# A fused attention and feed-forward kernel: attention-times-value matmuls of four head groups in one run, with attention weights reloaded per chunk

## The chip, the cores and the metric

The kernel runs on one core of a Trainium2 chip. The metric is the device time of one execution in microseconds (us); a figure for a kernel is the median of several executions. TensorE has two kinds of records in the traces, matmuls (PE) and weight loads (PEld).

## The reference

```python
# x [1, 2048, 576]; wqkv [576, 1728]; wo [576, 576]; w_gate, w_up [576, 4608]; w_down [4608, 576]; all bf16
xn = layernorm(x)
# A: 32 heads of 18, each query sees itself and the 255 keys before it
q, k, v = split(xn @ wqkv)
p = softmax(where(mask, q @ k.T * 18**-0.5, -1e9))
s = (p @ v) @ wo
# B: gated feed-forward
g = silu((sigmoid(xn @ w_gate) * (xn @ w_up)) @ w_down)
return x + s * g
```

## The kernel before

A host-side scheduler builds a list of operations per engine, simulates it with estimated durations and emits it unrolled: every matmul is an instruction of its own, there is no loop on the chip. The sequence of 2048 rows is cut into four chunks of 512. Attention (scores, exp, mask, then the product of probabilities and values, "PV") is fitted between the feed-forward matmuls, which are most of the work. Nearly all matmuls come in pairs that run at once, one on each row half of the array (in the trace of the kernel before, the two start 3 ns apart in the median, and at 512 columns the next pair starts 0.216 us later):

```python
def pair(eng, outs, lhs, rhs, start, stop, swap=0):            # L118
    for i in range(2):
        t = i ^ swap
        res = eng.matmul(outs[i], lhs(ROWS[t], i), rhs(ROWS[t], i), start=start, stop=stop, tile_position=(64 * t, 0))
```

Heads come in eight groups of four. A PV run takes two groups and one PSUM unit. Its matmuls use smaller tiles, 64 rows by 32 columns, eight at once (in the run at 163.89 us the eight of the first step start within 23 ns, and the next step 142 ns after the first's start):

```python
def build_pv(self, c, pr):                                     # L779, cut
    hp = self.pool_s.hold()                                    # one PSUM unit
    def f_pv(eng):
        outs = self.halves(hp, NT)
        for n, ks in enumerate(kss):                           # 12 key sub-blocks, 8 in chunk 0
            q0, q1 = span[ks]                                  # 1 to 5 query sub-blocks of 64
            cols = slice(q0 * SW, q1 * SW)
            for g, (hg, where, _) in enumerate(pend):          # 2 head groups
                for t in range(2):
                    for i in range(2):
                        res = eng.matmul(outs[i][p0:p0 + VH, cols], self.v_aug[ROWS[i], o:o + VH],
                                         self.expr[ROWS[i], se, t, cols], start=n == 0, stop=n == len(kss) - 1,
                                         tile_position=(64 * i, p0), skip_group_check=True)
    # ... then per half: transpose from PSUM, reciprocal, product, transpose back, DMA to oT
```

So a run is 12 x 8 = 96 matmuls in chunks 1 to 3 and 64 in chunk 0, with nothing else between them. There are 16 runs. The attention weights are loaded once and stay.

The softmax here doesn't subtract the row's maximum and nothing guards it: scores larger than these inputs give would overflow.

## Time and profile before

| | before |
|---|---|
| time, median (lowest to highest) | 559.01 us (558.83 to 559.52), 3 runs |
| span of the profiled run, granted clock | 557.7 us, 1.00 |
| PE busy | 552.4 us |
| next busiest engine (DVE) | 333.6 us |

The prediction below shows the lines that carry the reading of this profile. Two more views matter later. The first is the chain of work that ended last, in order of time (columns: start us, length us, engine, line, count). L801 is PV and L122 is `pair`.

```profile
163.96 1.27 PE ps L801 x89
165.23 22.82 PE ps L122 x246
188.05 1.27 PE ps L801 x87
```

A run passes through the chain in one piece, and the next feed-forward pair follows at once. The second view is the page's list of DMA queues (columns: packets, MB, share of 16 engines):

```profile
q1 hardware_dynamic: 105960, 60.68, 39.7%
q0 software_dynamic: 7424, 5.92, 4.0%
q8 instruction: 66, 1.08, 0.8%
```

Queue q8 is of the kind "instruction": 66 packets of 1.08 MB / 66 = 16.4 KB each.

### The profile page before, as it was taken

How to read it: one execution, taken by the hardware profiler on the slowest of the kernel's cores; microseconds unless marked ns; L12 is line 12 of the kernel's file. 1: busy time of each engine (PE TensorE's matmuls, PEld its weight loads, DVE VectorE, ACT ScalarE, POOL GpSimd, SP SyncE). 2: the span in 40 equal slices, each digit the busy share in tenths (PEclk: the TensorE clock that was granted, in tenths of full speed). 3: DMA queues.
4: the chain of work that ended last, by engine and by line, in shares of the span. 5: the costliest groups of instructions: out<-in, count | busy, mean ns of one | idle time of the engine just before them, and what ended most of it. 6: DMA issues, size and time to landing. Idle time of an engine off the chain costs nothing.

```text
span 557.7 us, 19262 instructions
## 1 busy us (share of the span) xinstructions
PE 552.4 (99%) x8342; PEld 339.1 (61%) x8342; DVE 333.6 (60%) x797; ACT 274.3 (49%) x383; POOL 210.3 (38%) x360
## 2 busy tenths in 40 slices
PE   8999999999999999999999999999999999999997
PEld 7454444677755545457886555645588754444787
DVE  5477788787568667674558757357567623333133
ACT  4245654443656655645656464565756433223011
POOL 5564456566245454440667434034382200000000
PEclk9999999999999999999999999999999999999999
DMA  7988997831125535534121264234511035552010
GB/s 217 323 234 190 223 264 211 213 58 45 53 73 155 159 108 145 142 108 96 29 63 44 72 192 123 82 117 140 171 31 38 24 115 148 169 151 68 2 45 24
DMA packets 113468, 67.83 MB, mean 122 GB/s; under 512 B 18620, under 2 KB 111516, under 8 KB 113384
## 3 DMA queue, kind: packets, MB, share of 16 engines
q1 hardware_dynamic: 105960, 60.68, 39.7%
q0 software_dynamic: 7424, 5.92, 4.0%
q8 instruction: 66, 1.08, 0.8%
q14 instruction: 18, 0.15, 0.1%
HBM read 55.15 MB, written 2.36 MB: 103 GB/s over the span
## 4 chain that ended last, share of the span: by engine, by line
PE 98%; DVE 1%; DMA 0%; issue 0%; DVEq 0%
PE ps L122 95%; PE ps L801 3%; DMA x<-in_A_x_dram 0%; DVE small L525 0%; DVE small L527 0%; DVE xnr L541 0%; PE ps L599 0%; DVE s_attn L1062 0%; DVE thf L1067 0%; DVE xnr L545 0%; DVE small L529 0%; DVE small L531 0%; DVE xf L1072 0%; DVEq L1227 0%
## 5 line engine op out<-in xcount | busy, mean ns | idle before, releaser
L122 PE MATMUL ps<-xnT,wgs 64*128 64x512 bf16 (+1 forms) x2400 | 282.6, 368 | 0.2
L751 ACT ACTIVATE expr<-ps 128x1024 bf16<-128x1024 f32 (+4 forms) x160 | 154.9, 969 | 77.8 <-PE ps L122 77.2
L122 PEld LDWEIGHTS ps<-xnT,wgs 64*128 64x128 bf16 x2400 | 113.9, 94 | 115.0 <-DVE hT L949 1.6
L122 PE MATMUL ps<-wd_sb,hT 64*128 64x288 bf16 (+2 forms) x2448 | 156.7, 276 | 0.0
L949 DVE SCALAR_TENSOR_TENSOR hT<-tring,ps 128x512 bf16<-128x512 bf16 x144 | 98.3, 683 | 94.7 <-ACT tring L946 93.6
L946 ACT ACTIVATE tring<-ps 128x512 bf16<-128x512 f32 x144 | 86.1, 598 | 129.6 <-PE ps L122 127.5
L122 PEld LDWEIGHTS ps<-wd_sb,hT 64*128 64x128 bf16 x2448 | 112.5, 94 | 28.5
L279 POOL DMA_DIRECT2D qk<-qd x160 | 82.2, 521 | 119.9 <-PE ps L122 109.6
L764 DVE TENSOR_TENSOR expr<-expr,mask 128x128 bf16<-128x128 bf16 (+2 forms) x240 | 63.6, 299 | 62.3 <-ACT expr L751 61.7
L715 POOL TENSOR_SCALAR kx<-kprev,small 128x256 bf16<-128x256 bf16 x64 | 61.3, 967 | 28.2 <-PE ps L122 27.4
L122 PE MATMUL ps<-qk,kx 64*128 64x320 bf16 (+1 forms) x704 | 59.4, 254 | 0.0
L279 POOL DMA_DIRECT2D oT<-o2T x72 | 36.4, 513 | 58.7 <-DVE o2T L827 49.8
L122 PE MATMUL ps<-xnT,wgr 64*128 64x512 bf16 (+1 forms) x300 | 56.0, 367 | 0.0
L122 PEld LDWEIGHTS ps<-qk,kx 64*128 64x128 bf16 x704 | 31.2, 94 | 21.5 <-ACT expr L751 0.6
L122 PE MATMUL ps<-xnT,wqk 64*128 64x512 bf16 x256 | 32.6, 376 | 0.0
L1052 ACT ACTIVATE thf<-ps 128x576 bf16<-128x576 f32 (+3 forms) x22 | 11.4, 519 | 39.7 <-PE ps L122 39.4
L819 DVE STREAM_TRANSPOSE ot<-ps 128x512 f32<-128x512 f32 x32 | 22.4, 700 | 11.6 <-PE ps L801 11.5
L715 DVE TENSOR_SCALAR kx<-qk,small 128x512 bf16<-128x512 bf16 x64 | 22.4, 378 | 4.7 <-PE ps L122 4.1
L122 PEld LDWEIGHTS ps<-xnT,wgr 64*128 64x128 bf16 x300 | 14.9, 94 | 16.5
L827 DVE STREAM_TRANSPOSE o2T<-o 128x512 bf16<-128x512 bf16 x32 | 22.7, 711 | 1.0
L637 DVE CAST qd<-ps 128x1024 bf16<-128x1024 f32 (+1 forms) x20 | 22.1, 1111 | 1.5 <-PE ps L122 1.5
L697 ACT ACTIVATE v_aug<-ps 64x288 bf16<-64x288 f32 x32 | 13.1, 409 | 17.3 <-PE ps L122 16.8
(71 smaller groups left out, 300.9 us busy)
## 6 DMA issues: line engine op xcount, KB each, us to landing
wgs<-in_B_w_gate_dram SPq DMA_DIRECT2D x72, 256.0 KB, 3.3
wgs<-in_B_w_up_dram SPq DMA_DIRECT2D x72, 256.0 KB, 3.9
wd_sb<-in_B_w_down_dram SPq DMA_DIRECT2D x9, 576.0 KB, 6.3
qk<-qd POOLq DMA_DIRECT2D x100, 36.0 KB, 2.6
wgr<-in_B_w_gate_dram SPq DMA_DIRECT2D x36, 64.0 KB, 2.3
wgr<-in_B_w_up_dram SPq DMA_DIRECT2D x36, 64.0 KB, 2.7
xf<-in_A_x_dram SPq DMA_DIRECT2D x16, 144.0 KB, 2.6
out_dram<-xf SPq DMA_DIRECT2D x15, 144.0 KB, 1.8
```

The costliest lines, as they stand in the source:

```text
L122: res = eng.matmul(outs[i], lhs(ROWS[t], i), rhs(ROWS[t], i), start=start, stop=stop, tile_position=(64 * t, 0))
L279: o = self.op(eng, DMA_ISSUE_NS[eng], lambda e: e.dma_start(dst, src), name, deps, prio, nbytes=nbytes)
L637: return eng.tensor_copy(dst, self.both(h, n))
L697: return eng.activation(dst, src, ACTF.Copy)
L715: return e.tensor_scalar(self.kx[:, sx, pos:pos + n_ // SW, t, :], src.rearrange("p (s k) -> p s k", k=SW), self.half[:, t:t + 1], None, A ...
L751: return eng.activation(self.expr[:, se, :, lo * SW:NT], self.both(h, NT)[:, :, lo * SW:NT], ACTF.Exp, scale=SM_SCALE)
L764: return eng.tensor_tensor(e_, e_, m_, ALU.mult)
L801: res = eng.matmul(outs[i][p0:p0 + VH, cols], self.v_aug[ROWS[i], o:o + VH], self.expr[ROWS[i], se, t, cols], start=n == 0, stop=n == len( ...
L819: return e.transpose(self.ot1[:, p1, :], self.halves(hp, NT)[i])
L827: t2 = op("DVE", dve_ns(NT), lambda e, p2=p2, p3=p3: e.transpose(self.o2T[:, p3, :], self.o2[:, p2, :]), f"ot2:{c}:{pr}:{i}", deps=[on, d3 ...
L946: th = op("ACT", act_ns(NT), lambda e: e.activation(self.tring[:, st, :], bank(h, 0), ACTF.Tanh, scale=0.5), f"th:{c}:{ft}", deps=[pg, dt_ ...
L949: mu = op("DVE", dve_ns(NT), lambda e: e.scalar_tensor_tensor(self.hT[:, ft, :], self.tring[:, st, :], 1.0, bank(h, 1), ALU.add, ALU.mult) ...
```

## The change

The intent is to halve the number of PV runs, because TensorE loses about a quarter of a microsecond around each (0.214 us in chunk 0 and 0.265 us later, read from the trace of the kernel before). Four head groups need 20 exp buffers in place of 12. The room comes from keeping only small buffers for the attention weights, reloading them in each chunk, and normalizing in place. The spacing of the score visits was tuned anew.

```diff
-NEX = 12
+NEX = 20
+NWQ = 2
+PVG = 2
-NQD = 2
+NQD = 1
+EVAC = (1, 0)
-SPACE_NS = ((1500, 1500, 1400, ...
+SPACE_NS = ((2200, 1700, 1500, ...
 ... (cut: buffers)
-        self.wqk, _ = seq("wqk", [P, KB - 1, 2, D])
-        self.wv_sb, _ = seq("wv_sb", [P, KB - 1, D])
-        self.wo_sb, _ = seq("wo_sb", [P, KB - 1, D])
+        self.wqk, _ = seq("wqk", [P, NWQ, KB - 1, 2, P])
+        self.wvo, _ = seq("wvo", [P, KB - 1, D])
 ... (cut: the remainders of these buffers)
-        self.xr, _ = seq("xr", [P, NXR, D])
 ... (cut: loads of q/k per column group, of v and o per chunk, LN in place)
-        if hg % 2:
-            self.build_pv(c, hg // 2)
+        if hg % (2 * PVG) == 2 * PVG - 1:
+            self.build_pv(c, hg // 2 - PVG + 1)
 ...
-        hp = self.pool_s.hold()
+        hp = self.pool_s.hold(PVG)
+        hps = hp.split()
 ...
-            outs = self.halves(hp, NT)
-            for n, ks in enumerate(kss):
+            for u, n, ks in [(u, n, ks) for u in range(PVG) for n, ks in enumerate(kss)]:
+                outs = self.halves(hps[u], NT)
-                for g, (hg, where, _) in enumerate(pend):
+                for g, (hg, where, _) in enumerate(pend[2 * u:2 * u + 2]):
```

There are now eight PV runs of 192 matmuls (128 in chunk 0).

## The prediction

> **What bounds the kernel now.** I read the page first: the busy shares, then the chain that ended last.

> ```profile
> PE 552.4 (99%) x8342; PEld 339.1 (61%) x8342; DVE 333.6 (60%) x797; ACT 274.3 (49%) x383; POOL 210.3 (38%) x360
> ...
> PE 98%; DVE 1%; DMA 0%; issue 0%; DVEq 0%
> PE ps L122 95%; PE ps L801 3%; DMA x<-in_A_x_dram 0%; DVE small L525 0%; DVE small L527 0%; DVE xnr L541 0%; PE ps L599 0%; DVE s_attn L1062 0%; DVE thf L1067 0%; DVE xnr L545 0%; DVE small L529 0%; DVE small L531 0%; DVE xf L1072 0%; DVEq L1227 0%
> ```

> The chain is TensorE from 7.3 us to 554.6 us; the next engine is busy only 60%. But the matmuls' recorded times overlap (the groups give a 512-column matmul 376 ns, the sum of all would exceed the span), so "99%" does not say that the array streams all the time. I therefore looked at starts. This is the timeline of TensorE around one PV run of a later chunk (columns: start us, length us, engine, line, operation, count):

> ```profile
> 162.93 0.81 PE L122 MATMUL ps<-xnT,wgs 64*128 64x512 bf16 x6
> 163.58 0.38 PE L122 MATMUL ps<-xnT,wgr 64*128 64x512 bf16 x2
> 163.89 1.34 PE L801 MATMUL ps<-expr,v_aug 64*19 64x320 bf16 x96
> 165.16 0.34 PE L122 MATMUL ps<-qk,kx 64*128 64x64 bf16 x4
> ```

> and around one of the first chunk:

> ```profile
> 63.00 0.59 PE L122 MATMUL ps<-xnT,wgs 64*128 64x512 bf16 x4
> 63.44 0.38 PE L122 MATMUL ps<-xnT,wgr 64*128 64x512 bf16 x2
> 63.74 1.01 PE L801 MATMUL ps<-expr,v_aug 64*19 64x320 bf16 x64
> 64.69 0.31 PE L122 MATMUL ps<-qk,kx 64*128 64x320 bf16 x2
> ```

> What to see: from 162.93 to 163.58 there are three pairs (the two of a pair run at once), so a 512-column pair takes 0.216 us start to start, that is 512 columns at 0.417 ns and 2.5 ns more. Taking this price for every pair in the trace, I summed how much later each next matmul starts than it could. Outside the PV runs, after the first 10 us, only about 1 us is left over in the whole span (two gaps of 0.23 us at 22.8 and 45.3 us are the largest). The array is full; time can only come from work that is itself less, from gaps at the PV runs, or from the start.

> **The gaps at the PV runs.** In a later chunk the pair before the run ends its turn at 163.58 + 0.216 = 163.796; the score matmul after it starts at 165.16: 1.364 us. The run has 12 steps, each of 8 matmuls at once, with 64 x (1+2+3+4+5+5+5+5+4+3+2+1) = 2560 columns: 2560 x 0.417 + 12 x 2.5 ns = 1.10 us. So 0.265 us is overhead: 0.094 at the entry (163.89 - 163.796), the rest inside and at the exit (I read about 0.142 at the exit, 0.03 within). In chunk 0 there are 8 steps and 1920 columns, 0.82 us of stream, and 64.69 - 63.656 = 1.034 us of time: 0.214 of overhead, 0.093 and 0.116 of it at the ends. Sixteen runs lose 4 x 0.214 + 12 x 0.265 = 4.0 us.

> [...] PV uses 64 rows x 32 columns (outputs of 19 partitions at 0, 32, 64, 96), all else 64 x 128. [...] one such change in, one out, 0.21 to 0.24 us together, and no such gap between other matmuls. [...] in this trace no run is held up measurably (the waits list TensorE's weight loads of L801 at 3.3 us of "issue" in 10 cases, at most 0.4[...] and 1.5 us on the mask line L764). [...] By the allocations, the kernel before takes 212.7 KB, about 207.7 KiB[...]. [...] the records here show 34 ns mean for a 256 B packet, 29 for 512 B, 59 for 1152 B: small packets cost over twice as much per byte.

> **The change part by part.**
> PV in one run on two units: the same matmuls, 8 runs in place of 16. Each merge takes away one exit and one entry, 0.21 us in chunk 0 (2 merges) and 0.235 us later (6 merges): 0.42 + 1.41 = 1.83 us, all of it on the path, since TensorE is the path. The 0.03 us inside a run stays.
> Twenty exp buffers: 8 more of 2048 B, 16.4 KB. Freed: q/k, v and o weights 22.0 KB, the raw x tiles 2.3 KB, half of qd 2.0 KB; new: small q/k buffers 4.6 KB and one v/o buffer 5.2 KB. Net 16.6 KB. It just fits. But four head groups have 4 x 5 = 20 visits: there is no spare buffer now (12 against 10 before). Visit 21 waits for the PV run, PV for the last exp (1.02 us) and its mask (0.3 to 0.43), and for both score units; after it both units need two transposes of 0.70 us with a normalization between (2.15 us for one transpose, reciprocal, product, transpose back). So at each of the 8 merges scores stand still for an estimated 4 to 6 us. This is covered by feed-forward matmuls, provided there are any: after the last PV run at 440 us there are 114 us of pure L122, so the attention runs a whole chunk ahead, and slowing it by 8 x 5 us moves nothing at the end. The wider spacing sums likewise: 5 visits x (54.4 - 49.0) us = 27 us more attention, well under 114.
> Reloads: 2.6 MB once becomes four times, 8.0 MB more on 67.8; q/k columns now in 256 and 128 B rows. Per chunk some 5900 small packets x 34 ns and 1280 others x 54 ns are 270 us of engine time, 17 us of 16 engines; four chunks less the 9 us of before is an estimated 58 us, spread over 450 us. The share goes from about 45% to some 55%. Off the path where the transfer is asked for early.
> Issues on the SP queue: some 100 more at about 0.55 us, hidden. LN in place, one qd buffer, one v/o buffer: added ordering, no added engine work; five small DVE copies go. No TensorE work is added.
> Sum: 559.0 - 1.8, plus an allowance of 0.1 us in four or so places where a wait now shows, gives 557.3.

> **The rivals.**
> (1) New waits at the PV run eat the gain. Both score units, one of which also serves the feed-forward, are held together for the run (2.3 us) and for up to two normalizations. Then feed-forward has two units: each takes 1.94 us of matmuls (9 pairs), and its tanh (0.60) and product (0.69) plus a possible transpose ahead on DVE (0.72) take 2.3 us with the hops. That would stall TensorE up to 0.4 us a few times per merge, 3 to 6 us in all, and the time would be 558 to 562. Against it: before, scores and PV also occupied both units around a run and no stall shows.
> (2) Weights late in the first 100 us. The windows show the transfers there near their ceiling (columns: window, length, busy us and count of PE, PEld, DVE, ACT, POOL, clock, DMA share, GB/s):

> ```profile
> 20.00:40.00 20.00, 19.93 (x218) 10.28 (x216) 12.30 (x28) 6.73 (x14) 9.95 (x21) 1.00 1.00 275
> 40.00:60.00 20.00, 19.93 (x202) 9.38 (x200) 16.21 (x49) 10.95 (x17) 7.73 (x14) 1.00 0.77 176
> 60.00:80.00 20.00, 20.00 (x266) 9.98 (x262) 16.21 (x45) 11.64 (x18) 12.20 (x21) 1.00 1.03 256
> ```

> Chunk 0 now fetches q/k in short rows there, about 8 us more of DMA time over 90 us. For it: 1.00 of share. Against: the first 40 us ask for fewer bytes than before (two of five column groups in place of all), and the shares stay under what the queue carried at 323 GB/s in one slice. Worth +1 to +3 us if it comes.
> (3) The gain is larger than the drain, because wider spacing also removes the remaining small gaps. There is only about 1 us of them: 556 at best.

> **Range and chances.** Faster by over 2% would need 547.8, which nothing here can give with a full array; slower by over 2% would need 11 us of stalls, more than rivals 1 and 2 in their middle size. The range 555.8 to 559.6 takes in the full drain with some small gaps below, and rival 1 or 2 at a third of its size above.

> **What would show it.** Right: 8 groups of 192 (128 in chunk 0) matmuls of L801 in the chain, each about 2.45 us long (1.85 in chunk 0), TensorE otherwise without gaps, the mean spacing unchanged, attention ending later than 440 us, some 76 MB moved. Wrong: gaps of 0.1 us or more ahead of L801 or of feed-forward pairs just after it, waited for on DVE lines L764, L819 or L949, would be rival 1; gaps ended by weight transfers before 110 us would be rival 2. The prediction is also wrong if the change of tile between the two halves of a merged run drains too, for then no time is saved at all.

Where passages are cut, the cut is marked: they gave rules and a figure that no trace or run shows. 559.0 - 1.83 for the eight merges, plus 0.1 us for waits that show, gives 557.3 us; the 1.83 us are worked out from the measured 0.21 and 0.235 us per merge. That the buffers' room is used up, the reason given for freeing some, was not shown; the sum of 16.4 KB needed and 16.6 KB freed stands without it. "Drain", in the prediction and in the expectations, is the time lost where the tiles change, and the traces show that time alone.

## The result, and the profile after

| | before | after |
|---|---|---|
| time, median (lowest to highest), same chip | 559.08 us (558.83 to 559.52), 4 runs | 573.65 us (573.24 to 574.92), 4 runs |
| span of the profiled run, granted clock | 557.7 us, 1.00 | 572.0 us, 0.997 |

The ratio is 1.0264, with a 95% interval of 1.0246 to 1.0282: slower by 2.6%. The prediction of 557.3 us, with a range up to 559.6, was wrong.

First the page of the kernel after (busy times, DMA totals, the main queue and the chain by engine). L823 is PV and L129 is `pair`:

```profile
PE 554.1 (97%) x8342; PEld 348.8 (61%) x8342; DVE 331.2 (58%) x792; ACT 273.7 (48%) x383; POOL 209.0 (37%) x360
...
DMA packets 141341, 75.87 MB, mean 133 GB/s; under 512 B 43804, under 2 KB 139388, under 8 KB 141256
...
q1 hardware_dynamic: 133832, 68.71, 44.9%
...
PE 96%; issue 2%; DVE 1%; DMA 0%; DVEq 0%
```

The number of matmuls is the same, 8342, and PE is busy for nearly the same time. What is new is "issue", 2% of the chain: time in which TensorE waited for nothing that the profile shows. The chain in order of time shows where it lies (columns as before):

```profile
135.47 1.79 PE ps L823 x124
137.26 0.23 PE ps L129 x2
137.49 1.47 issue
138.96 63.82 PE ps L129 x740
202.78 1.72 PE ps L823 x118
204.50 2.01 issue
206.51 0.90 PE ps L823 x48
207.40 2.07 PE ps L129 x17
```

The run at 202.78 is broken in two by 2.01 us of nothing. The timeline of TensorE there (columns: start us, length us, engine, line, operation, count, idle time before) puts numbers on it:

```profile
202.39 0.38 PE L129 MATMUL ps<-xnT,wgr 64*128 64x512 bf16 x2
202.71 1.79 PE L823 MATMUL ps<-expr,v_aug 64*19 64x320 bf16 x137
206.51 0.90 PE L823 MATMUL ps<-expr,v_aug 64*19 64x256 bf16 x55 [2.01 <-issue]
207.33 1.04 PE L129 MATMUL ps<-xnT,wgs 64*128 64x512 bf16 x8
```

The 137th matmul starts at 204.23 (its neighbours overlap it, so the row's length is longer) and the 138th at 206.51. Nothing in the program separates these two; they are of one kind, in one run, and the program waits for all their data before the run, not inside it. The waits of TensorE (columns: engine and line, what was waited for, us in total, times, longest) sum up the whole span:

```profile
PE ps L823 <- issue: 10.0, 6, 2.8
PE ps L129 <- issue: 2.0, 2, 1.5
```

Six runs of eight stop inside, and one, the second of chunk 0, just behind its end (137.49). Only the first run has none. Taking the starts of matmuls (the method of the prediction), and a run's 0.205 us of overhead without a stop (measured in e2_align below), the seven stops cost 1.65, 2.23, 0.73, 2.50, 2.94, 1.32 and 1.65 us: **13.0 us**. (The expectations below count the idle time between records instead, 11.4 us.)

### A theory: the program does not arrive in time

What do seven places have in common, when none of them waits for data? I numbered TensorE's instructions in program order: one for every weight load, matmul and semaphore record. The kernel after has 16,941 of them, and q8 has 66 packets: 256.7 instructions to a packet. The other kernels agree: e2_align below has 18,033 instructions and 70 packets (257.6), e6_before_dense 19,721 and 77 (256.1). So I counted in blocks of 256.

In this numbering **all seven stops lie at place 192 or 193 of 256**. Since that one place holds for all, it is taken as the block's end; the first 64 instructions of the first block would then be ones without a record, which is an inference. From here on "crossing" is TensorE reaching such a place. These are the times of the stops in the kernel after, with the start of the q8 packet that comes between:

```
crossing   next crossing reached   q8 packet starts   TensorE goes on
 135.40          137.19                136.58              138.96
 202.85          204.23                204.03              206.51
 255.15          256.58                254.92              257.36
 313.62          315.02                314.95              317.36
 369.55          371.09                371.43              374.05
 436.02          437.39                436.46              438.79
 487.96          489.40                488.17              491.10
```

By the theory the density of the instructions decides. Each matmul is two instructions, its weight load and itself (8342 of each on the page). A feed-forward pair is four in 0.216 us, so 256 last 13.8 us. A PV run is 384 instructions in 2.40 us, so 256 last 1.6 us. Before, a run was 192 instructions: any 256 that held a whole run held at least 64 others too, 2.0 to 3.5 us of feed-forward (pairs of 288 or of 512 columns). Merging two runs made 384 in a row. By the theory a run that holds two crossings stops; the experiments test that.

### The rest of the difference

After the stop at 315 us the granted clock fell. This is the table of windows (columns: window, length, busy us and count of PE, PEld, DVE, ACT, POOL, clock, DMA share, GB/s):

```profile
315.00:317.30 2.30, 0.29 (x30) 0.10 (x10) 0.00 (x0) 0.00 (x0) 0.02 (x1) 1.00 0.38 108
317.36:318.30 0.94, 0.94 (x53) 0.84 (x52) 0.00 (x0) 0.00 (x0) 0.00 (x0) 0.79 0.00 0
318.37:321.60 3.23, 3.23 (x25) 1.12 (x18) 2.39 (x5) 0.60 (x1) 0.00 (x0) 0.54 0.02 5
321.60:325.00 3.40, 3.33 (x36) 1.47 (x34) 2.86 (x6) 1.22 (x2) 0.00 (x0) 1.00 0.06 16
```

In the third window seven feed-forward pairs took 0.40 to 0.43 us each in place of 0.216: 2.96 - 7 x 0.216 = 1.45 us. In each of the eleven traces all changes of the clock lie whole multiples of 3.413 us apart, and the half clock here lasts 3.413 us, from 317.91 to 321.32. Cut into windows on that grid, the traces have, inside their spans, six windows (in four traces) in which TensorE was idle for 1.92 to 2.51 us by its records, and each was followed by a window at half clock; no window with up to 1.89 us was. So in these traces it depends on where a stop falls. The one at 315 us lay in one window (2.07 us idle), the longer one at 371 us was cut by a window's end (1.24 and 1.52 us) and was followed by 1.00.

The sum, before to after: stops +13.03, half clock +1.45, the first 11 us +1.19 (of which 0.69 is a gap at instruction 449, again place 193 of 256; in the kernel before the first 11 us have 1.75 us of gaps, here 2.94), the runs' tile changes -1.86. That is 13.81 of the 572.04 - 557.68 = 14.36 us between the two profiles. The other 0.55 us are small waits.

### The profile page after: what moved, and what is told of

Same layout as the page of the kernel before. It is cut to its first block, busy times and chain, and to the rows that moved or that the text cites. A ratio compares the mean times of both kernels' runs of the same rounds, so it can differ in the third digit from the quotient of the medians.

```text
span 572.0 us, 19381 instructions
## 1 busy us (share of the span) xinstructions
PE 554.1 (97%) x8342; PEld 348.8 (61%) x8342; DVE 331.2 (58%) x792; ACT 273.7 (48%) x383; POOL 209.0 (37%) x360
## 2 busy tenths in 40 slices
DMA packets 141341, 75.87 MB, mean 133 GB/s; under 512 B 43804, under 2 KB 139388, under 8 KB 141256
## 3 DMA queue, kind: packets, MB, share of 16 engines
q1 hardware_dynamic: 133832, 68.71, 44.9%
## 4 chain that ended last, share of the span: by engine, by line
PE 96%; issue 2%; DVE 1%; DMA 0%; DVEq 0%
PE ps L129 92%; PE ps L823 3%; DMA x<-in_A_x_dram 0%; DVE small L523 0%; DVE small L525 0%; PE ps L595 0%; DVE xnr L539 0%; DVE s_attn L1086 0%; DVE thf L1091 0%; DVE xnr L543 0%; DVE small L527 0%; DVE small L529 0%; DVE xf L1096 0%; DVEq L1251 0%
## 5 line engine op out<-in xcount | busy, mean ns | idle before, releaser
L129 PE MATMUL ps<-xnT,wgs 64*128 64x512 bf16 (+1 forms) x2400 | 287.0, 369 | 0.8 <-issue 0.5
L129 PEld LDWEIGHTS ps<-xnT,wgs 64*128 64x128 bf16 x2400 | 117.7, 94 | 111.9 <-issue 3.9
L129 PE MATMUL ps<-wd_sb,hT 64*128 64x288 bf16 (+2 forms) x2448 | 155.1, 276 | 1.5 <-issue 1.5
L129 PEld LDWEIGHTS ps<-wd_sb,hT 64*128 64x128 bf16 x2448 | 114.4, 94 | 28.9 <-issue 1.7
L129 PE MATMUL ps<-qk,kx 64*128 64x320 bf16 (+1 forms) x704 | 59.9, 254 | 0.0
L129 PE MATMUL ps<-xnT,wgr 64*128 64x512 bf16 (+1 forms) x300 | 56.8, 369 | 0.0
L129 PEld LDWEIGHTS ps<-qk,kx 64*128 64x128 bf16 x704 | 33.2, 94 | 24.1 <-ACT expr L776 0.9
L129 PE MATMUL ps<-xnT,wqk 64*128 64x512 bf16 (+1 forms) x320 | 37.8, 355 | 0.1
L1076 ACT ACTIVATE thf<-ps 128x576 bf16<-128x576 f32 (+3 forms) x22 | 11.4, 520 | 50.0 <-PE ps L129 49.7
L823 PE MATMUL ps<-expr,v_aug 64*19 64x320 bf16 (+4 forms) x1408 | 19.9, 255 | 10.0 <-issue 10.0
L744 POOL COPY kprev<-qk 128x256 bf16<-128x256 bf16 x32 | 12.6, 401 | 38.2 <-DVE kx L740 36.9
L823 PEld LDWEIGHTS ps<-expr,v_aug 64*19 64x19 bf16 x1408 | 17.3, 87 | 14.1 <-issue 12.3
L129 PEld LDWEIGHTS ps<-xnT,wgr 64*128 64x128 bf16 x300 | 15.5, 94 | 16.1 <-issue 0.3
```

Source lines behind the costliest of these rows:

```text
L744: self.op_kp[hg] = op("POOL", 420, lambda e: e.tensor_copy(self.kprev[:, hg, :], self.qk[:, qs, 1, NT // 2:NT]), f"kp:{c}:{hg}", deps=[kxo ...
L1076: return e.activation(v2(t)[:, a:b, :], y2()[:, a:b, :], ACTF.Tanh, scale=0.25)
```

## The experiments

All results were correct. The runs e1 to e4 share a before of 558.87 us, e5 to e7 one of 558.89, e8 and e9 one of 558.95. To move crossings without moving data, an edit called padding below splits some feed-forward pairs into two halves over their columns, well ahead of a PV run. That adds four instructions per pair and hardly any array time, and shifts all that follows by four places:

```diff
+    if SPLIT[0] and not start:
+        SPLIT[0] -= 1
+        n = outs[0].shape[-1] // 2
+        for a in (0, n):
+            for i in range(2):
+                t = i ^ swap
+                res = eng.matmul(outs[i][:, a:a + n], lhs(ROWS[t], i), rhs(ROWS[t], i)[:, a:a + n],
+                                 start=False, stop=stop and a > 0, tile_position=(64 * t, 0))
+        return res
```

Places below are a run's first instruction, modulo 256, in the numbering of above (crossing at 192).

### e1_pvg1: the change without the merge

```diff
-PVG = 2
-EVAC = (1, 0)
+PVG = 1
+EVAC = (0,)
```

> The changed kernel with its PV runs cut back to two head groups on one PSUM unit; 20 exp buffers, reloads, in-place LN and new spacing stay. Theory F (TensorE's program arrives in blocks of 256 instructions, and a run of 384 instructions in 2.2 us uses a block up faster than the next one comes): the seven stops (11.4 us) and the eight slow pairs (1.7 us) go, eight drains (1.8 us) come back: 560 to 563 us, no idle time of over 0.4 us inside or just behind a PV run. Rival B (both PSUM units and all 20 exp buffers held by one run make waits): falls too, this run does not tell B from F. Rival D (the reloads and the reuse of single buffers cost the time): stays at 571 to 574 us.

Measured: 561.29 us (560.46 to 561.69), 1.0045 [1.0028, 1.0062]. This is within F's range. The trace has no stop at a crossing. Reloads, single buffers, the larger exp ring and the new spacing together cost 2.4 us; the merge is the cause of the rest.

### e2_align: the whole change, with runs shifted to begin just behind place 0

```diff
+PV_PAD = (0, 33, 52, 60, 5, 25, 42, 56)     # pairs split ahead of each run: 273
```

The runs then start at 94, 64, 2, 3, 2, 1, 4, 2.

> The changed kernel with its order, runs and buffers untouched; only some feed-forward matmul pairs well ahead of each PV run go out as two halves (4 instructions more each, 273 pairs, about 2.5 ns each, 0.7 us in all), so that each run of 384 instructions starts at place 2 of 256 by my count and holds one block end (place 192) instead of two. Theory F: stops of under 3 us in all instead of 11.4, time 561 to 565 us. Rivals B and D: nothing that they speak of has changed, 573 to 575 us.

Measured: 559.12 us (558.89 to 559.93), 1.0006 [0.9991, 1.0021], better than expected. All stops are gone, though the kernel executes 1092 more instructions, moves the same data and keeps the same waits. The timeline of the run that was broken in the kernel after:

```profile
200.30 0.39 PE L143 MATMUL ps<-xnT,wgr 64*128 64x512 bf16 x2
200.62 2.46 PE L837 MATMUL ps<-expr,v_aug 64*19 64x320 bf16 x192
203.02 1.04 PE L143 MATMUL ps<-xnT,wgs 64*128 64x512 bf16 x8
```

Now 192 matmuls go through in one piece of 203.02 - 200.62 = 2.40 us. Their stream is 24 steps, 2 x 1.10 = 2.19 us; so a merged run carries 0.205 us inside and at its exit. A run of 96 in the kernel before carries 0.178, so the change of PSUM unit in the middle costs 0.03 us at most.

### e3_misalign: the control, nearly as many splits, but runs placed to hold two crossings

```diff
+PV_PAD = (0, 0, 37, 60, 5, 26, 41, 56)      # 225 pairs; runs start at 94, 188, 66, 67, 66, 69, 68, 66
```

> As the aligned one, with 227 pairs cut in two, but each run of 384 starts at place 66 to 69, so that it holds two block ends, the second just at its end. Theory F: six stops of 2 to 3 us (the run that started at place 69 in the changed kernel stopped for 2.8 us) and the stop of the first chunk: 14 to 19 us of stops, 576 to 582 us. Rivals B and D: the same time as the aligned one, 573 to 575 us.

Measured: 575.56 us (574.40 to 576.37), 1.0296 [1.0281, 1.0312], just under what F expected (225 pairs were split in the end, not 227). This is the list of TensorE's waits:

```profile
PE ps L837 <- issue: 11.7, 6, 3.3
PE ps L143 <- issue: 1.5, 1, 1.5
```

All six runs of chunks 1 to 3 stop inside and the second of chunk 0 behind, all at place 192 or 193. Two of the stops were followed by 3.41 us of half clock, at 207 and 320 us. So it is not the splitting that helped in e2_align, but the place: 225 splits at wrong places give 575.6 us, 273 at right ones 559.1.

### e4_split: all buffers and units of the change, but the run cut in two, 4 us apart

```diff
-        pv = op("PE", est, f_pv, f"pv:{c}:{pr}", ..., acq=hp)
+        pv = op("PE", est, lambda eng: f_pv(eng, 0), f"pv:{c}:{pr}", ..., acq=hp)
+        pv = op("PE", est, lambda eng: f_pv(eng, 1), f"pv2:{c}:{pr}", odeps=[pv], prio=1)   # at least 4000 ns later
```

The rival theory B is the prediction's first rival: both PSUM units and all 20 buffers are held together, and that causes the waits. Here they are held even longer.

> The changed kernel with the PV run of four head groups cut in two by 4 us or so of other matmuls; it still waits for all 20 masks and both PSUM units first, and all buffers and both units come free only after the second half. Theory F: no run has more than 192 instructions in a row, so the stops go, eight drains come back: 560 to 564 us. Rival B: the buffers and units are held even longer than in the changed kernel, 574 us or more. Rival D: 573 to 576 us.

Measured: 564.32 us (563.97 to 564.69), 1.0097 [1.0082, 1.0112], 0.3 us above F's range and 10 below B's. First the timeline of TensorE around one pair of halves, then its waits:

```profile
209.10 1.35 PE L824 MATMUL ps<-expr,v_aug 64*19 64x320 bf16 x96
210.38 1.04 PE L130 MATMUL ps<-xnT,wgs 64*128 64x512 bf16 x8
...
213.66 1.03 PE L130 MATMUL ps<-xnT,wgs 64*128 64x512 bf16 x8
214.61 1.34 PE L824 MATMUL ps<-expr,v_aug 64*19 64x320 bf16 x96
```
```profile
PE ps L130 <- DVE hT L975: 1.2, 2, 0.8
```

Each half is whole, 1.28 us to the next matmul as in the kernel before, and no stop stands at a crossing. B's wait, feed-forward pairs waiting for DVE to free a unit, is there: 1.2 us in two places, with eleven of the pauses of 0.23 us in which TensorE waits for itself between the halves of a feed-forward tile. So B is real and worth a few us where the units are held longer, but it is not what made the change slow.

### e5_scan: at which places does a run of 384 stop?

```diff
+PV_PAD = ...   # 241 pairs; runs start at 94, 188, then 30, 31, 226, 109, 224, 130
```

> Again the changed kernel with feed-forward pairs cut in two ahead of the runs (241 pairs), so that the six runs of 384 start at places 30, 31, 226, 109, 224, 130 of 256: which starts stop, and for how long. Theory F: every stop is at place 192 or 193. Starts 109 and 130 hold two block ends (83 and 339, 62 and 318 instructions in): a stop of 1.5 to 3 us each. Starts 30 and 31 have the second end 34 or 33 instructions behind the run, about 1.8 us of feed-forward after a first end 1.3 us before the run's last instruction: a stop of under 1.5 us. Starts 224 and 226 have ends 32 before and 222 in: 1.7 us before the run and 1.3 us into it, 0 to 1.5 us. In all 4 to 9 us of stops, 562 to 568 us. Rivals B and D are out already and expect nothing here.

Measured: 568.08 us (565.72 to 569.18), 1.0158 [1.0129, 1.0186], at the upper edge of F's range. Stops, all at 192 or 193: starts at 109 and 130 stop for 2.74 and 1.93 us, 188 (256 instructions) for 1.76; 226 and 224 not at all; 30 not and 31 for 0.68. The arithmetic explains the sides. From 109 or 130 the second crossing falls 339 or 318 instructions after the start, inside the run. From 226 it falls 478 after the start, 94 instructions behind the run. At 30 and 31 it falls 34 and 33 behind. That is near the edge: behind the run from 31 come down-projection pairs of 288 columns, which use up instructions faster, 32 a us in place of 18.5 (four in 0.1225 us in place of 0.216), so its crossings are 2.34 us apart and those of the run from 30 are 3.09.

### e6_before_dense: the kernel before, made denser in instructions alone

```diff
-                            res = eng.matmul(outs[i][p0:p0 + VH, cols], ...)
+                            m_ = (q0 * SW + q1 * SW) // 2
+                            for a, b in ((q0 * SW, m_), (m_, q1 * SW)):
+                                res = eng.matmul(outs[i][p0:p0 + VH, a:b], ..., start=n == 0 and a == q0 * SW, ...)
```

No merge, no reload, no new buffer: each PV matmul is cut in two over its columns, so a run of two groups has 384 instructions.

> The kernel before, with nothing of the change, but each PV matmul goes out as two over half the columns: the same arithmetic, twice the instructions, so each run of two head groups has 384 (256 in the first chunk) in a row. Theory F: the stops appear here too, at place 192 or 193 and in those runs that hold two block ends (starts 168, 96, 73, 111, 146, 98, 153) and behind the last run of the first chunk (start 184): 8 stops of 1 to 3 us, some 16 us, beside a longer run itself from the denser issue, 0.5 to 1 us each for 12 to 16 runs: 575 to 595 us. If the stops came from holding two units, twenty buffers or the reloads, there would be none here: 565 to 573 us.

Measured: 597.90 us (593.98 to 599.88), 1.0689 [1.0641, 1.0737], slightly above the range. The timeline of one run:

```profile
168.69 1.56 PE L803 MATMUL ps<-expr,v_aug 64*19 64x160 bf16 x140
172.02 0.67 PE L803 MATMUL ps<-expr,v_aug 64*19 64x160 bf16 x52 [1.77 <-issue]
172.62 0.39 PE L122 MATMUL ps<-qk,kx 64*128 64x64 bf16 x6
```

The kernel before now shows the same fault as the kernel after: 14 stops of 0.4 to 2.6 us, all at place 192 or 193. The seven runs for which two crossings had been computed beforehand (starts 168, 96, 73, 111, 146, 98, 153) all stopped inside. Part of the added time is another thing: a run without a stop takes 1.886 us in place of 1.277, for the same columns in twice as many matmuls. The difference of 0.61 us in 16 runs would be at most 9.8 us, less in chunk 0. The profiled run is 592.7 - 557.7 = 35.0 us longer, and its 14 stops sum to some 23 us, so with a mean clock of 0.994 the rest is accounted for.

### e7_align_few: the same with fewer splits

```diff
+PV_PAD = (0, 21, 0, 0, 0, 25, 41, 0)        # 87 pairs; runs start at 94, 16, 2, 19, 254, 253, 252, 26
```

> The aligned kernel with fewer pairs cut (87 in place of 273): the long runs start at places 2, 19, 254, 253, 252, 26. Theory F, if that much of a shift is still clear of stops: 0.5 us less than the aligned one, 558.0 to 559.5 us; if starts 19 or 26 stop, 560 to 561 us.

Measured: 560.52 us (559.66 to 561.56), 1.0030 [1.0015, 1.0045], the second of the two outcomes: behind the runs from 19, 252 and 26 TensorE stopped, for 0.45, 0.42 and 1.15 us. From 252 this was not expected.

### e8_best: all starts moved to 222 to 254

```diff
+PV_PAD = (0, 13, 0, 0, 0, 28, 39, 0)        # 80 pairs; runs start at 94, 240, 226, 243, 222, 233, 224, 254
```

> The changed kernel with 80 feed-forward pairs cut in two, so that the long runs start at places 222 to 254, where the scan and the run before it saw no stop (224, 226, 252 to 254). Theory F: no stop over 0.3 us at any of the six long runs, 558.0 to 559.5 us, level with the kernel before or up to 0.15% below it; the first 11 us can add up to 1 us either way. If the block ends just ahead of the runs matter, 560 to 563 us.

Measured: 559.33 us (558.97 to 560.27), 1.0009 [0.9997, 1.0021]. The time is in the range expected, level with the kernel before and not below it. But one stop was left in the profiled run, the slowest of the five, where none over 0.3 us was expected:

```profile
360.49 1.53 PE L837 MATMUL ps<-expr,v_aug 64*19 64x320 bf16 x108
362.85 1.18 PE L837 MATMUL ps<-expr,v_aug 64*19 64x192 bf16 x84 [0.83 <-issue]
```

This run starts at 233, so its two crossings are 3.54 us apart, which elsewhere sufficed; but here the packet of q8 began only 2.2 us after the first crossing. How late the packet starts varies, and no run shows why (see "Left open").

### e9_reload_only: reloads and single buffers alone, with the spacing and 12 exp buffers of before

```diff
-NEX = 20
-PVG = 2
+NEX = 12
+PVG = 1
 SPACE_NS = (that of the kernel before)
```

> The change without its PV part: reloaded weights in small buffers, normalization in place, one qd buffer, but PV of two head groups, 12 exp buffers and the spacing of the kernel before. What the reloads and the single buffers cost alone. Rival D: at least half of what the cut-back kernel lost (2.4 us), 560 to 562 us. If the reloads are hidden, as the prediction had it: 558.5 to 559.7 us.

Measured: 560.71 us (560.43 to 562.88), 1.0042 [1.0029, 1.0054]: 2.35 us by the ratio, as rival D had it. The reloads and single buffers are not free. The waits of TensorE show only small items, such as these:

```profile
PE ps L129 <- DVE qd L660: 0.3, 1, 0.3
PE ps L129 <- DVE hT L973: 0.3, 1, 0.3
```

These two and a few pauses of 0.24 to 0.5 us at feed-forward pairs are spread over the span. Which of the reloads, the single buffers and the normalization in place makes them stays open.

### What was not tried on the chip

Taking away TensorE's wait for itself of 0.23 us between the halves of a feed-forward tile was not run. Nothing shows what it would gain, or whether the result would stay correct.

### All crossings together

I took every interval between two crossings in the traces of all eleven kernels, leaving out the first 20 us or so, and asked whether TensorE then stopped by 0.38 us or more:

| time from one crossing to the next | stopped | went through |
|---|---|---|
| under 2.3 us | 29 (0.38 to 3.5 us) | 0 |
| 2.3 to 3.6 us | 6 | some 25 |
| over 3.6 us | 1 (4.44 us, packet 2.7 us late) | all others |

In the first 20 us four kernels (after, e5_scan, e7_align_few and e8_best) stopped too, at the end of the second block, for 0.3 to 1.2 us, though 4.2 to 4.5 us had passed since the crossing before. There too the packet had started late, 2.4 to 3.0 us after that crossing.

The kernel before never has less than 3.04 us, and it never stops. The shortest in e2_align is 2.99. The kernel after has seven under 1.8.

## Why the prediction was wrong

**The array as the bound, and the cost of a tile change: right.** In e2_align the overhead of two separate runs, 2 x (0.178 inside and at the exit + 0.094 at the entry) = 0.544 us, became 0.205 + 0.095 = 0.30 in a later chunk, and 2 x (0.121 + 0.093) = 0.43 became 0.153 + 0.093 = 0.246 in chunk 0. Six times 0.245 and twice 0.18 is 1.83 us, the predicted figure; that it agrees to the last digit is partly luck, since the predicted terms were 0.235 and 0.21 and their errors cancel. The price it rests on, 0.417 ns a column and 2.5 ns a matmul, comes out of the trace: pairs of 512 and of 288 columns follow each other by 0.2158 and 0.1225 us. A merged run without a stop takes 2.40 us (1.79 in chunk 0), against 2.45 (1.85) predicted. The fear that the change of unit inside a run would cost as much as leaving and entering did not come true (0.205 us against 0.178).

**The step that failed.** It is the step "the same matmuls, 8 runs in place of 16", with its conclusion "No TensorE work is added". The work is the same, but the order is not. The prediction priced columns, tile changes, buffers and bytes, and never counted instructions. 384 of them within 2.40 us can hold two block ends, and wherever two lay under 2.3 us apart TensorE stopped (29 of 29). That took 13.0 us in stops and 1.45 us in the half clock that followed one of them. Moving the runs' places takes both away: between e2_align and e3_misalign, which differ in the place of the splits and by 48 splits, lie 16.4 us. The sentence "All of it on the path, since TensorE is the path" carried the risk too: with PE busy for 99% of the span before, the stops came on top of the time and make 13.03 of the 14.36 us.

**Twenty exp buffers and both units (rival 1): right in kind, not the cause.** Attention did end later, the last run at 488 us in place of 439, and nothing at the end moved. The waits on DVE that the prediction named appear in e4_split, for 1.2 us, where the units are held longest. The gaps of the kernel after had no such releaser, so by the prediction's own list of signs neither of its first two rivals had happened, and the kernel was slower all the same. When all listed rivals are absent, the list was too short.

**Reloads: bytes right, time low, effect mis-sized.** "Some 76 MB" moved: 75.87. The estimated 58 us of 16 engines was too high: queue q1 went from 39.7% of 557.7 us (221) to 44.9% of 572.0 (257), 35 us. The sums of the spacing are 48.6 and 54.1 us, not 49.0 and 54.4, which changes its 27 us of slower attention by half a us and nothing else. The allowance for waits that show, 0.1 us in four or so places, should have been 2.4 us (e9_reload_only). So even without stops the merge, 1.83 us, no more than pays for the room that it needs. That fits e2_align and e8_best, which equal the kernel before; none of the kernels beats it.

**Weights late in the first 100 us (rival 2): not seen.** The first 11 us did lengthen by 1.19 us, 0.69 of it at a block end.

**Left open:** why the packet starts at a varying time after a crossing, and which part of the reloads costs the 2.4 us. On the first the traces show a tendency only. At the 111 crossings with the DMA engines busy for 90% or more of the 2 us around them, the packet starts 1.2 us after the crossing on average, at those with under 60% some 0.2 us. Single packets don't follow it (one in e7_align_few started 1.5 us late with the engines idle), and no run tested it. Every execution was traced, so whether an untraced one stops as long isn't shown.

## What to carry to other kernels

Count the instructions of a dense stretch, not only its columns: in these runs a stretch that used up 256 TensorE instructions in under 2.3 us always stopped, and one that took over 3.6 us did so once (the first 20 us left out). So in a kernel like this one a run of small tiles is best kept to less than 256 instructions, with large matmuls around it (192 in the kernel before, which never stops at a crossing), or placed so that it doesn't hold two block ends, as in e2_align (559.12 us in place of 573.65). A gap that the profile calls "issue", in the middle of a run of like matmuls, is to be checked against the program's place modulo 256 before any data is suspected. When a change has to buy its room elsewhere, price what is given up as carefully as what is gained: here 1.8 us of gain met 2.4 us of cost before any stop.
